# A gated-linear-attention kernel with a SoLU feed-forward: z in natural column order for four chunks, a row-permuted second copy of w_out, two raw weight buffers, and a new written order

## The chip, the cores and the metric

One core of a Trainium2 chip runs the whole kernel. The metric is the time of one execution on the device in microseconds (us), the median of several runs. Lower is better.

## The reference, cut to what matters

Inputs q, k, v, a_re and a_im have the shape (4, 8, 768, 48): 4 sequences (batch), 8 heads, 768 time steps, 48 values per head. The first half is a recurrence with a complex gate whose modulus is cut at 0.999; y of all heads, 384 wide, is the input x of a feed-forward with d_ff = 1024:

```
S_re, S_im = new_re + kv, new_im            # new = a_n * S, kv = outer(k_t, v_t)
y[t] = q_t @ S_re
...
h = x @ w_in                                # (3072, 384) @ (384, 1024)
sm = exp(h - max) / sum(exp(h - max))
solu = h * sm
ln = (solu - mean) / sqrt(var + 1e-06) * g_ln
out = ln @ w_out                            # (3072, 1024) @ (1024, 384)
```

The weights arrive as 64-bit numbers and are turned into fp32 in the kernel.

## The kernel before, in words

**Tiling.** The 3072 rows are 24 chunks of 128 rows: 6 stretches of time by 4 sequences, so chunks 0 to 3 are the first stretch. Two chunks make a group (12 groups). A helper closure exists for each small step of each group or chunk, and the string ORDER (L517) is a list of them, "step:number", written out by hand. The program walks through that list (L1314) and issues each step's instructions. No scheduler moves anything afterwards, so ORDER fixes the sequence of every engine and of the DMA queue of SyncE (SP), which issues nearly all transfers. An instruction waits only for what it reads, and for the buffer that it overwrites to be free.

**Steps of a group** (prep_steps): load_ar and load_ai; inverse, ratio, sure, tangent, square, secant, fourth, size, eps, lnm take the logarithm of the modulus and the tangent of the angle by turns on ScalarE (ACT) and VectorE (DVE); group 0 does each of them in two halves, a and b. total0/1 are products with a triangle of ones (running sums over time, tile f_L); grow and decay are their exponentials; a table load ("trig"), angle, phase0/1 (products again), nearest, part, cos and sin follow, then a table load back ("exp"). From group 3 on the products use a high and a low part in fp32r: lh and ll for total, xh and xl for phase. "on" adds the phase of the stretch before, which "onward" sends over as a transfer, and "last" sends the last row of decay to f_rows.

**Steps of a chunk:** ks and qs scale k and q; k2 and q2 double them with cos and sin; then they are transposed: for chunks 0 and 1 by the tensor engine (kt, qt, copied back by kT, qT), for the rest by DVE in 32x32 blocks (kqb) and four transfers (kqt0). score0/1, mask0 and values give y, carry and add update the state. turned_x copies y; up0/1 are the product with w_in (48 instructions, L1115); exp0 (L1125) writes z = exp(h) from the PSUM tile f_h; solu0 (L1134) multiplies it by h and sums it; centred, spread and norm make mean and variance; z is transposed; down0/1 (L1192) are the product with w_out; scale and store finish.

**The order of z's columns.** For most chunks z is transposed by DVE in 32x32 blocks (blocks, L1152) and by four transfers, one for each block of 32 rows (away, L1157), which spread 32 partitions by 4 column blocks over 128 partitions. So partition p = 4f + s of the result holds column 32s + f of a block of 128. The rows of w_out have to lie the same way: fetch (L742) loads them permuted, and "gain" loads g_ln permuted with four transfers. For the chunks in SHORT (0, 1, 2 and 23) z is transposed whole by the tensor engine (zt, copied by zT), so there exp0 writes z itself in the permuted order: column 32s + f goes to place 4f + s. Then solu0 is four instructions with 256 columns each and centred adds up four sums.

**Weights.** There are 7 pieces: 0 to 2 of w_in (1024 columns each), 3 to 6 of w_out (2 x 384 columns). fetch loads a piece into a buffer of the pool f_raw (3 buffers), raised (ACT, L748) and convert (DVE, three instructions from L754) make fp32 of it, with a tile "bits" between them. mean, meansum and centre fold g_ln and a mean into w_out. "again" loads each piece a second time at the end for inspect (L761), which looks at its smallest size; judge, judgew, judges and count (L1271) make a flag of all checks, and if it isn't zero a general version (function general) runs afterwards. It did not run here. Low parts ll and xl also take buffers of f_raw.

## Time and profile before

| | us |
|---|---|
| median of 3 runs | 418.93 |
| lowest and highest | 418.43 and 420.42 |
| the profiled execution, its own time | 420.45 |
| the profiled execution, first to last instruction (span) | 418.5 |
| tensor engine (PE) busy | 380.5 |
| DVE busy | 341.9 |
| ACT busy | 303.4 |
| GpSimd (POOL) busy | 79.3 |

A row of the profile names the line, the engine, the operation, and the tiles as out<-in; x24 is the number of instructions; then follow the busy time, the mean of one in ns, and the idle time of the engine ahead of it with what ended it. In the timeline the first column is the start, the second the length. PEld is the load of weights into the tensor engine, SPq the issue of a transfer on SP. Matmuls of fp32 count twice, since each is issued as two.

### The profile page before, as it was taken

The numbers are of one execution on the slowest core, as the hardware profiler recorded it, in microseconds if no ns is written. First come the engines' busy times: TensorE is split into PE (matmuls) and PEld (weight loads), VectorE is DVE, ScalarE is ACT, GpSimd is POOL, SyncE is SP. The second block draws the span as 40 slices with busy tenths as digits, with TensorE's granted clock in tenths as the row PEclk, the third lists the DMA queues.
The fourth block names the chain that finished last, engine by engine and source line by source line (L and its number), as shares of the span: only waits on it lengthen the run. The fifth ranks groups of instructions, "written<-read, shape, count | busy, mean of one in ns | idle before, by whom it ended". The sixth has DMA issues, their size and how long they took to land.

```text
span 418.5 us, 15922 instructions
## 1 busy us (share of the span) xinstructions
PE 380.5 (91%) x6968; PEld 206.0 (49%) x6968; DVE 341.9 (82%) x438; ACT 303.4 (73%) x487; POOL 79.3 (19%) x148
## 2 busy tenths in 40 slices
PE   0258769999999999999999999999999999999993
PEld 0026234534655645654654744645645646545552
DVE  4898799888898898898888899989989887963441
ACT  5997887796796887787788778877877967721440
POOL 3000000313222122131122232212304122110110
PEclk9999999999999999999999999999999999999998
DMA  8998338596678667877788858778679669478761
GB/s 228 283 268 227 66 77 172 121 238 125 157 143 185 167 141 144 216 164 146 178 192 186 191 110 198 177 183 207 145 181 211 133 142 217 94 181 258 218 239 30
DMA packets 167406, 72.60 MB, mean 173 GB/s; under 512 B 142496, under 2 KB 155936, under 8 KB 166560
## 3 DMA queue, kind: packets, MB, share of 16 engines
q1 hardware_dynamic: 167040, 71.07, 71.5%
q8 instruction: 57, 0.93, 1.0%
q10 hardware_dynamic: 288, 0.43, 0.3%
q14 instruction: 21, 0.17, 0.1%
HBM read 38.87 MB, written 4.72 MB: 104 GB/s over the span
## 4 chain that ended last, share of the span: by engine, by line
PE 79%; ACT 7%; DVE 5%; DMA 5%; SPq 2%; issue 1%; ACTq 0%; DVEq 0%
PE f_h L1115 27%; PE f_o L1192 25%; PE f_y L1074 9%; PE f_score L1041 6%; PE f_d L1082 3%; DMA out_dram<-f_ot 2%; PE f_L L863 2%; PE f_phase L863 2%; PE f_o L1202 1%; DVE f_kb L996 1%; DVE f_z L1134 1%; PE f_phase L868 1%; DMA f_ar<-in_a_re_dram 1%; PE f_turned L1008 1%; DMA f_k<-in_k_dram 1%
## 5 line engine op out<-in xcount | busy, mean ns | idle before, releaser
L1115 PE MATMUL f_h<-f_w_in,f_xT 128*32 128x512 f32 x1152 | 131.8, 598 | 0.0
L1192 PE MATMUL f_o<-f_w_out,f_zT 128*32 128x384 f32 x1472 | 124.1, 487 | 0.1
L1192 PEld LDWEIGHTS f_o<-f_w_out,f_zT 128*32 128x32 f32 x1472 | 50.8, 110 | 63.1 <-issue 61.8
L1115 PEld LDWEIGHTS f_h<-f_w_in,f_xT 128*32 128x32 f32 x1152 | 40.2, 111 | 66.0 <-issue 65.5
L996 DVE STREAM_TRANSPOSE f_kb<-f_kq 128x1536 f32<-128x1536 f32 x22 | 56.2, 2555 | 0.8 <-DMA f_kqT<-f_kb 0.3
L1125 ACT ACTIVATE f_z<-f_h 128x1024 f32<-128x1024 f32 x24 | 28.8, 1202 | 25.8 <-PE f_h L1115 25.6
L1134 DVE SCALAR_TENSOR_TENSOR f_z<-f_h,f_z 128x1024 f32<-128x1024 f32 (+1 forms) x36 | 33.8, 970 | 11.8 <-ACT f_z L1125 11.6
L1179 POOL TENSOR_SCALAR f_s<-f_s,f_sum 128x1 f32<-128x1 f32 x24 | 12.9, 537 | 149.6 <-ACT f_z L1173 149.5
L1074 PE MATMUL f_y<-f_att,f_v 128*32 128x128 f32 (+1 forms) x384 | 37.0, 278 | 1.1 <-DVE f_att L1046 1.1
L1074 PE MATMUL f_y<-f_att,f_vr 128*32 128x128 f32 x384 | 37.3, 278 | 0.0
L1046 DVE TENSOR_TENSOR f_att<-f_score,f_mats 128x1024 f32<-128x1024 f32 x24 | 29.2, 1215 | 9.7 <-PE f_score L1041 9.7
L1041 PEld LDWEIGHTS f_score<-f_kqT 96*32 96x32 f32 x1536 | 32.2, 112 | 8.2 <-issue 8.1
L1041 PE MATMUL f_score<-f_kqT 96*32 96x32 f32 (+3 forms) x1536 | 33.2, 238 | 0.0
L1074 PE MATMUL f_y<-f_kqT,f_state 96*32 96x128 f32 (+1 forms) x640 | 33.1, 272 | 0.0
L1173 ACT ACTIVATE f_z<-f_z,f_less 128x1024 f32<-128x1024 f32 x24 | 27.3, 1138 | 0.0
L856 POOL TENSOR_TENSOR f_ll<-f_lr,f_lh 128x768 fp32r<-128x768 f32 x9 | 16.6, 1848 | 55.0 <-ACT f_lh L851 48.2
L1074 PEld LDWEIGHTS f_y<-f_att,f_v 128*32 128x32 f32 (+1 forms) x384 | 23.1, 105 | 7.1 <-issue 4.3
L1074 PEld LDWEIGHTS f_y<-f_att,f_vr 128*32 128x32 f32 x384 | 23.2, 112 | 4.8 <-issue 4.8
L1152 DVE STREAM_TRANSPOSE f_zb<-f_z 128x1024 f32<-128x1024 f32 x20 | 24.7, 1237 | 0.1
L1219 ACT ACTIVATE f_ot<-f_o,f_rs 128x384 f32<-128x384 f32 x23 | 13.1, 571 | 14.6 <-PE f_o L1192 6.5
L987 DVE TENSOR_TENSOR f_kq<-f_cs,f_k 128x768 f32<-128x768 f32 x24 | 22.9, 952 | 0.4 <-ACT f_cs L941 0.2
L987 DVE TENSOR_TENSOR f_kq<-f_cs,f_q 128x768 f32<-128x768 f32 x24 | 22.9, 953 | 0.0
(116 smaller groups left out, 628.5 us busy)
## 6 DMA issues: line engine op xcount, KB each, us to landing
f_kqT<-f_kb SPq DMA_DIRECT2D x88, 192.0 KB, 3.3
f_zT<-f_zb SPq DMA_DIRECT2D x80, 128.0 KB, 3.0
f_raw<-in_moe_w_out_dram SPq DMA_DIRECT2D x16, 384.0 KB, 4.6
f_raw<-in_moe_w_in_dram SPq DMA_DIRECT2D x6, 1024.0 KB, 7.9
f_k<-in_k_dram SPq DMA_DIRECT2D x12, 384.0 KB, 5.2
f_q<-in_q_dram SPq DMA_DIRECT2D x12, 384.0 KB, 4.6
f_v<-in_v_dram SPq DMA_DIRECT2D x12, 384.0 KB, 5.4
out_dram<-f_ot SPq DMA_DIRECT2D x23, 192.0 KB, 3.2
```

What stands on the lines that cost most here:

```text
L863: nc.tensor.matmul(out=ps, lhsT=tri.bitcast(FR), rhs=st[nm][:, i * DM:(i + 1) * DM], start=(k == 0), stop=(k == len(parts) - 1))
L987: nc.vector.tensor_tensor(out=t, in0=T["cs", g][:, i * H:(i + 1) * H], in1=heads(T[nm, g][:, i]).unsqueeze(2).to_broadcast([P, H, 2, D]), ...
L996: nc.vector.transpose(out=t, in_=T["kq", c].rearrange("p n h (f j) -> p j (n h) f", j=3))
L1041: nc.tensor.matmul(out=scores[r0:r0 + 32, x, r:], lhsT=QK[:, r // 32, x], rhs=QK[:, r // 32:, H + x], start=True, stop=True)
L1046: nc.vector.tensor_tensor(out=st["att"].rearrange("p (i u) t -> p i u t", u=2), in0=scores.rearrange("p (i u) t -> p i u t", u=2), in1=mat ...
L1074: nc.tensor.matmul(**product)
L1115: nc.tensor.matmul(out=st["h"][r:r + 32, half * 512:(half + 1) * 512], lhsT=st["xT"][:, c * P + r:c * P + r + 32], rhs=w_in[:, c, half * 5 ...
L1125: nc.scalar.activation(out=z, in_=h, func=AF.Exp, accum_out=sums[:, n:n + 1])
L1134: nc.vector.scalar_tensor_tensor(out=z, in0=h, scalar=1.0, in1=z, op0=OP.mult, op1=OP.mult, accum_out=st["sum"][:, 2 + i:3 + i])
L1152: nc.vector.transpose(out=st["zb"], in_=st["z"].rearrange("p (c s f) -> p s c f", s=4, f=32))
L1173: nc.scalar.activation(out=st["z"], in_=st["z"], func=AF.Square, bias=st["less"], accum_out=st["sum"][:, 1:2])
L1192: nc.tensor.matmul(out=st["o"][rows], lhsT=zT, rhs=w_out[:, c], start=(c == 0), stop=(c == KF - 1))
```

## The change

- exp0, solu0 and centred have one form for all chunks: z is in natural order.
- w_out and g_ln are loaded in natural order (g_ln with one transfer). After centring, "mixed" copies w_out in two halves, four transfers each, from SBUF to SBUF into a new tile w_mix with its rows permuted. down uses w_out for the chunks in SHORT, w_mix for the others.
- f_raw has 2 buffers instead of 3. The first loads of pieces 0 and 3 go to the memory of w_mix instead, before it has its own content. The pool "bits" is gone: the bits lie in the tile zb. The low parts ll and xl lie in the tile "f", which the phases of the group also use. judge writes its comparison in place.
- ORDER is another list: the same steps and the two of mixed, in another sequence. Its name init:0 stands for nothing. The tiles of the last down have another name.

The diff; ORDER, which changes as a whole, is cut to its start, a middle piece and its end.

```diff
@@ -514,91 +514,91 @@
 ORDER = """
-load_ara:0 inversea:0 load_aia:0 ratioa:0 surea:0 load_arb:0 tangenta:0 inverseb:0 squarea:0 load_aib:0 secanta:0
-fourtha:0 ratiob:0 sureb:0 sizea:0 fetch:5 epsa:0 tangentb:0 squareb:0 secantb:0 lnma:0 fetch:1 raised:5 load_k:0
-sizeb:0 fetch:0 epsb:0 total0:0 convert:5 load_q:0 fourthb:0 raised:1 grow0:0 decay0:0 lnmb:0 total1:0 grow1:0 fetch:2
-decay1:0 convert:1 trig:0 anglea:0 angleb:0 ks1:0 phase0:0 phase1:0 load_vr:0 raised:0 convert:0 nearest0:0 nearest1:0
-load_ar:1 part0:0 cosa:0 sina:0 qs0:0 qs1:0 load_ai:1 part1:0 ks0:0 sinb:0 fetch:6 cosb:0 q2:0 last:0 exp:0 qt0:0
-qT0:0 raised:2 k2:0 qt1:0 qT1:0 kt0:0 kt1:0 load_v:0 q2:1 convert:2 kT0:0 inverse:1 fetch:3 fetch:4 gain:0 kT1:0 qt1:1
...
-store:20 spread:22 up1:23 inspect:3 norm:22 down0:22 exp0:23 down1:22 again:2 again:1 solu0:23 zt0:23 centred:23
-scale:22 zT0:23 zt1:23 spread:23 down0:23 norm:23 judges:0 zT1:23 inspect:1 store:21 inspect:2 down1:23 scale:23
-store:22 store:23 inspect:4 judgew:0 down2:23 count:0 scale2:23 store2:23 flag:0
+init:0 load_aia:0 load_ara:0 inversea:0 load_arb:0 ratioa:0 load_aib:0 surea:0 load_q:0 tangenta:0 fetch:5 fetch:1
+inverseb:0 squarea:0 ratiob:0 secanta:0 sureb:0 sizea:0 load_v:0 tangentb:0 epsa:0 load_k:0 lnma:0 squareb:0 secantb:0
+fourthb:0 sizeb:0 total0:0 epsb:0 fourtha:0 raised:5 lnmb:0 decay0:0 grow0:0 total1:0 grow1:0 decay1:0 fetch:0 trig:0
+anglea:0 convert:5 phase0:0 last:0 raised:1 qs0:0 angleb:0 convert:1 phase1:0 nearest0:0 part0:0 turn_ends:0
+nearest1:0 ks0:0 ks1:0 sina:0 cosa:0 load_ai:1 qs1:0 part1:0 q2:0 tot:0 sinb:0 k2:0 cosb:0 exp:0 qt1:0 load_ar:1 qT1:0
+raised:0 q2:1 kt1:0 k2:1 convert:0 kT1:0 inverse:1 ratio:1 kt0:0 qt0:0 qT0:0 kT0:0 fetch:2 score1:0 fetch:6 qt0:1
+qT0:1 load_vr:0 score0:0 qt1:1 sure:1 raised:2 load_q:1 mask0:0 values:0 tangent:1 kt1:1 fetch:3 square:1 secant:1
+turned_x:0 convert:2 qT1:1 up0:0 fetch:4 raised:6 size:1 eps:1 convert:6 lnm:1 fourth:1 onward:0 up1:0 gain:0 total1:1
+load_k:1 kT1:1 raised:3 exp0:0 grow1:1 total0:1 decay0:1 grow0:1 carry:1 convert:3 solu0:0 decay1:1 trig:1 angle:1
+kt0:1 phase1:1 ks1:1 qs0:1 kT0:1 add:1 phase0:1 ks0:1 score1:1 raised:4 nearest0:1 score0:1 nearest1:1 convert:4
+part0:1 carry:0 part1:1 mean:0 mean:3 mean:7 add:0 sin:1 cos:1 mask0:1 load_q:2 q2:2 k2:2 mean:1 zt0:0 exp:1 load_ar:2
+mean:4 mean:2 inverse:2 values:1 mean:5 kqb:2 turned_x:1 load_ai:2 ratio:2 mean:6 zT0:0 meansum:0 again:5 last:1
...
+load_ar:3 decay1:2 kqb:3 trig:2 mixed:1 zt0:1 kqt0:3 last:2 values:2 angle:2 spread:0 zT0:1 on:2 phase1:2 ks1:2 norm:0
+qs0:2 turned_x:2 phase0:2 carry:2 load_ai:3 nearest1:2 nearest0:2 up0:2 part1:2 part0:2 sin:2 add:2 cos:2 ks0:2 k2:4
...
+store:18 down0:21 spread:21 solu0:22 again:0 values:23 inspect:4 down1:21 turned_x:23 up0:23 centred:22 up1:23 norm:21
+blocks:22 scale:21 away:22 again:2 down0:22 judge:0 exp0:23 store:21 inspect:0 again:6 spread:22 solu0:23 norm:22
+down1:22 zt0:23 zt1:23 judges:0 inspect:2 inspect:6 scale:22 zT0:23 judgew:0 centred:23 zT1:23 store:20 count:0 flag:0
+spread:23 down0:23 down1:23 norm:23 store:22 scale:23 store:23 down2:23 scale2:23 store2:23
 """
@@ -639,7 +639,7 @@
     const, ld, ldv = pool("f_const", 1), pool("f_ld", 2), pool("f_ldv", 3)
     tmp, one, two = pool("f_tmp", 1), pool("f_one", 1), pool("f_two", 2)
     natk, kbp = pool("f_natk", 2), pool("f_kb", 1)
-    rawp, bits = pool("f_raw", 3), pool("f_bits", 1)
+    rawp = pool("f_raw", 2)
     ffp, zp, sml = pool("f_ff", 2), pool("f_z", 2), pool("f_sml", 4)
     zbp = pool("f_zb", 1)
     ps_t = pool("f_ps_t", 2, space=PSUM)
@@ -654,6 +654,8 @@
     unit, quarter, small, mhalf, magic, mmagic, mone = (bias[:, i:i + 1] for i in range(7))
     w_in = const.tile([P, KD, FF], FP, name="f_w_in")
     w_out = const.tile([P, KF, DM], FP, name="f_w_out")
+
+    w_mix = const.tile([P, KF, DM], FP, name="f_w_mix")
     g_ln = const.tile([P, KF], FP, name="f_g_ln")
 
     state = [const.tile([D2, H // 2, P], FP, name=f"f_state{b}") for b in range(B)]
@@ -672,6 +674,8 @@
     least = const.tile([P, 7], FP, name="f_least")
     T, steps = {}, {}
 
+    EARLY = [0, 3]
+
     SHORT_KQ = [0, 1]
 
     SHORT = [0, 1, 2, 23]
@@ -732,19 +736,19 @@
 
         def fetch(i):
             w, wide, c, per, n = pieces[i % len(pieces)]
-            raw = T["raw", i] = rawp.tile([P, NW, 2], I32, tag="raw", name="f_raw")[:, 0:n]
+            if i in EARLY:
+                raw = w_mix.rearrange("p c x -> p (c x)")[:, 0:2 * NW].bitcast(I32).rearrange("p (n u) -> p n u", u=2)[:, 0:n]
+            else:
+                raw = rawp.tile([P, NW, 2], I32, tag="raw", name="f_raw")[:, 0:n]
+            T["raw", i] = raw
             for k in range(per):
-                rows = wide[:, c + k]
-                if w is w_out:
-
-                    rows = rows.rearrange("(s f) x -> f s x", s=4)
                 m = n // per
-                nc.sync.dma_start(out=raw[:, k * m:(k + 1) * m].rearrange("p n u -> p (n u)"), in_=rows)
+                nc.sync.dma_start(out=raw[:, k * m:(k + 1) * m].rearrange("p n u -> p (n u)"), in_=wide[:, c + k])
 
         def raised(i):
 
             n = pieces[i][4]
-            y = T["bits", i] = bits.tile([P, NW], I32, tag="bits", name="f_bits")[:, 0:n]
+            y = T["bits", i] = zbp.tile([P, NW], FP, tag="zb", name="f_bits")[:, 0:n].bitcast(I32)
             nc.scalar.activation(out=y, in_=T["raw", i][:, :, 0].bitcast(U32), func=AF.Copy, scale=2.0 ** -29)
 
         def convert(i):
@@ -782,7 +786,16 @@
             nc.vector.scalar_tensor_tensor(out=w_out[:, c], in0=w_out[:, c], scalar=g_ln[:, c:c + 1], in1=T["mean"],
                                            op0=OP.mult, op1=OP.subtract)
 
+        def mixed(half):
+
+            cs = slice(half * KF // 2, (half + 1) * KF // 2)
+            for s in range(4):
+                nc.sync.dma_start(out=w_mix[s:P:4, cs].rearrange("p c x -> p (c x)"),
+                                  in_=w_out[s * 32:s * 32 + 32, cs].rearrange("p c x -> p (c x)"))
+
         own = len(pieces)
+        for half in range(2):
+            steps["mixed", half] = partial(mixed, half)
         for i in range(own):
             steps["fetch", i], steps["again", i] = partial(fetch, i), partial(fetch, own + i)
             steps["raised", i], steps["convert", i] = partial(raised, i), partial(convert, i)
@@ -851,11 +864,11 @@
             nc.scalar.activation(out=t, in_=st[src], func=AF.Copy, scale=by)
 
         def low(nm, src, hi, by):
-            t = st[nm] = rawp.tile([P, 1024], FR, tag="raw", name="f_" + nm)
+            t = st[nm] = one.tile([P, GW], FR, tag="f", name="f_" + nm)
             if by == 1.0:
-                nc.gpsimd.tensor_tensor(out=t[:, 0:GW], in0=st[src], in1=st[hi].bitcast(FP), op=OP.subtract)
+                nc.gpsimd.tensor_tensor(out=t, in0=st[src], in1=st[hi].bitcast(FP), op=OP.subtract)
             else:
-                nc.vector.scalar_tensor_tensor(out=t[:, 0:GW], in0=st[src], scalar=by, in1=st[hi].bitcast(FP), op0=OP.mult,
+                nc.vector.scalar_tensor_tensor(out=t, in0=st[src], scalar=by, in1=st[hi].bitcast(FP), op0=OP.mult,
                                                op1=OP.subtract)
 
         def halves(ps, i, *parts):
@@ -1120,19 +1133,12 @@
         def exp():
             z = st["z"] = ffp.tile([P, FF], FP, tag="z", name="f_z")
             h = st["h"]
-            if n in SHORT:
-                z, h = z.rearrange("p (c f s) -> p c s f", s=4, f=32), h.rearrange("p (c s f) -> p c s f", s=4, f=32)
             nc.scalar.activation(out=z, in_=h, func=AF.Exp, accum_out=sums[:, n:n + 1])
 
         def solu():
-            st["sum"] = sml.tile([P, 6], FP, tag="sum", name="f_sum")
-            parts = [(st["h"], st["z"])]
-            if n in SHORT:
-                parts = [(st["h"].rearrange("p (c s f) -> p s c f", s=4, f=32)[:, s],
-                          st["z"].rearrange("p (c f s) -> p s c f", s=4, f=32)[:, s]) for s in range(4)]
-            for i, (h, z) in enumerate(parts):
-                nc.vector.scalar_tensor_tensor(out=z, in0=h, scalar=1.0, in1=z, op0=OP.mult, op1=OP.mult,
-                                               accum_out=st["sum"][:, 2 + i:3 + i])
+            st["sum"] = sml.tile([P, 2], FP, tag="sum", name="f_sum")
+            nc.vector.scalar_tensor_tensor(out=st["z"], in0=st["h"], scalar=1.0, in1=st["z"], op0=OP.mult, op1=OP.mult,
+                                           accum_out=st["sum"][:, 0:1])
 
 
         def turn_z(half):
@@ -1148,7 +1154,7 @@
 
 
         def blocks():
-            st["zb"] = zbp.tile([P, 4, KF, 32], FP, tag="zb", name="f_zb")
+            st["zb"] = zbp.tile([P, FF], FP, tag="zb", name="f_zb").rearrange("p (s c f) -> p s c f", s=4, f=32)
             nc.vector.transpose(out=st["zb"], in_=st["z"].rearrange("p (c s f) -> p s c f", s=4, f=32))
 
         def away():
@@ -1162,12 +1168,7 @@
 
         def centred():
             st["less"] = sml.tile([P, 1], FP, tag="less", name="f_less")
-            total = st["sum"][:, 2:3]
-            if n in SHORT:
-                half, total = st["sum"][:, 2:4], st["sum"][:, 0:1]
-                nc.gpsimd.tensor_tensor(out=half, in0=half, in1=st["sum"][:, 4:6], op=OP.add)
-                nc.gpsimd.tensor_tensor(out=total, in0=st["sum"][:, 2:3], in1=st["sum"][:, 3:4], op=OP.add)
-            nc.gpsimd.tensor_scalar(out=st["less"], in0=total, scalar1=-1.0 / FF, scalar2=None, op0=OP.mult)
+            nc.gpsimd.tensor_scalar(out=st["less"], in0=st["sum"][:, 0:1], scalar1=-1.0 / FF, scalar2=None, op0=OP.mult)
 
         def spread():
             nc.scalar.activation(out=st["z"], in_=st["z"], func=AF.Square, bias=st["less"], accum_out=st["sum"][:, 1:2])
@@ -1185,16 +1186,16 @@
                 st["o"] = ps_o.tile([P, DM], FP, tag="o", padded_shape=[P, 512], name="f_o")
             for c in range(half * KF // 2, (half + 1) * KF // 2):
                 if n in SHORT:
-                    parts = [(slice(r * 32, r * 32 + 32), st["zT"][:, c, r * 32:r * 32 + 32]) for r in range(4)]
+                    parts, w = [(slice(r * 32, r * 32 + 32), st["zT"][:, c, r * 32:r * 32 + 32]) for r in range(4)], w_out
                 else:
-                    parts = [(slice(r * 32, r * 32 + 32), st["zT"][:, r, c]) for r in range(4)]
+                    parts, w = [(slice(r * 32, r * 32 + 32), st["zT"][:, r, c]) for r in range(4)], w_mix
                 for rows, zT in parts:
-                    nc.tensor.matmul(out=st["o"][rows], lhsT=zT, rhs=w_out[:, c], start=(c == 0), stop=(c == KF - 1))
+                    nc.tensor.matmul(out=st["o"][rows], lhsT=zT, rhs=w[:, c], start=(c == 0), stop=(c == KF - 1))
 
         def down_last(part):
 
             if part == 0:
-                st["o"] = [pl.tile([P, DM // 2], FP, tag=tag, padded_shape=[P, 512], name="f_o") for pl, tag in ((ps_o, "o"), (ps_y, "y"))]
+                st["o"] = [pl.tile([P, DM // 2], FP, tag=tag, padded_shape=[P, 512], name="f_" + tag) for pl, tag in ((ps_o, "o"), (ps_y, "y"))]
             for x in ((0, 1), (0,), (1,))[part]:
                 cols = slice(x * DM // 2, (x + 1) * DM // 2)
                 for c in range(KF // 2) if part == 0 else range(KF // 2, KF):
@@ -1245,13 +1246,11 @@
     def judge():
 
         good = sml.tile([P, 2, NG + 1], FP, tag="good", name="f_good")
-        ends = rawp.tile([P, 512, 2], I32, tag="raw", name="f_ends").bitcast(FP).rearrange("p n u -> p (n u)")
-        ends = ends[0:GH, 0:NG * D].rearrange("p (g d) -> p g d", d=D)
         row = one_row()
         nc.vector.tensor_scalar(out=good[:, 0], in0=seen[:, 0], scalar1=MOST, scalar2=None, op0=OP.is_le)
         nc.vector.tensor_scalar(out=good[:, 1], in0=seen[:, 1], scalar1=SURE, scalar2=None, op0=OP.is_le)
         nc.vector.memset(row[:, 3:4], 0.0)
-        nc.vector.tensor_scalar(out=ends, in0=rows[:, :, 0], scalar1=LEAST, scalar2=None, op0=OP.is_ge, op1=OP.add,
+        nc.vector.tensor_scalar(out=rows[:, :, 0], in0=rows[:, :, 0], scalar1=LEAST, scalar2=None, op0=OP.is_ge, op1=OP.add,
                                 accum_out=row[0:GH, 3:4])
         nc.vector.tensor_reduce(out=row[:, 0:1], in_=good.rearrange("p a b -> p (a b)"), op=OP.add, axis=AX.X)
 
@@ -1299,8 +1298,7 @@
         for own in (turn_steps(c), chunk_steps(c), ffn_steps(c)):
             steps.update({(nm, c): f for nm, f in own.items()})
     def gain():
-        for s in range(4):
-            nc.sync.dma_start(out=g_ln[s:P:4], in_=moe_g_ln.rearrange("(c s f) -> f s c", s=4, f=32)[:, s])
+        nc.sync.dma_start(out=g_ln, in_=moe_g_ln.rearrange("(c p) -> p c", p=P))
 
     steps["gain", 0] = gain
     steps["judge", 0], steps["judgew", 0], steps["judges", 0] = judge, judge_weights, judge_sums
```

## The prediction

> **What bounds the kernel now.** I first read the share of each engine in 40 slices, then the busy time in stretches of 10 us, then the waits, and last the timelines of the first 106 us and the last 40. The slices show three parts:
>
> ```profile
> PE   0258769999999999999999999999999999999993
> DVE  4898799888898898898888899989989887963441
> ACT  5997887796796887787788778877877967721440
> ```
>
> TensorE (PE) is filled from the eighth slice to the last but one; before that VectorE (DVE) and ScalarE (ACT) are the full ones. In stretches (columns: length, then busy us of PE, PE loads, DVE, ACT, POOL, clock, DMA share, GB/s):
>
> ```profile
> 0.00:10.00 10.00, 0.00 (x0) 0.00 (x0) 4.10 (x16) 5.17 (x10) 3.48 (x11) 1.00 0.85 221
> 10.00:20.00 10.00, 3.02 (x16) 0.40 (x16) 8.01 (x12) 8.96 (x19) 0.00 (x0) 1.00 0.95 274
> 20.00:30.00 10.00, 5.29 (x27) 2.62 (x28) 9.57 (x14) 9.08 (x15) 0.00 (x0) 1.00 1.12 290
> ...
> 50.00:60.00 10.00, 6.29 (x178) 4.61 (x182) 8.82 (x19) 9.25 (x15) 0.61 (x3) 1.00 0.41 83
> 60.00:70.00 10.00, 8.93 (x131) 3.56 (x127) 9.89 (x12) 7.15 (x14) 0.00 (x0) 1.00 0.49 110
> ...
> 90.00:100.00 10.00, 8.58 (x142) 3.88 (x134) 7.31 (x14) 7.76 (x13) 3.95 (x6) 1.00 0.85 177
> 100.00:150.00 50.00, 50.00 (x980) 27.11 (x974) 44.23 (x53) 40.53 (x65) 11.06 (x18) 1.00 0.67 152
> ```
>
> Adding the ten stretches to 100 us, PE is idle for 31 us; from 100 to 406 it isn't idle at all. The change adds no matmul and takes none away. So it can win only in the start and the tail, and can lose anywhere. What it takes out is in these groups and, in the timeline, in the exp of chunk 1 and of chunk 3:
>
> ```profile
> L1134 DVE SCALAR_TENSOR_TENSOR f_z<-f_h,f_z 128x1024 f32<-128x1024 f32 x20 | 24.4, 1218 | 4.1 <-ACT f_z L1125 3.9
> L1134 DVE SCALAR_TENSOR_TENSOR f_z<-f_h,f_z 128x256 f32<-128x256 f32 x16 | 9.4, 661 | 7.6 <-ACT f_z L1125 7.6
> ...
> 72.23 2.14 ACT L1125 ACTIVATE f_z<-f_h 128x1024 f32<-128x1024 f32 x1
> ...
> 103.94 1.02 ACT L1125 ACTIVATE f_z<-f_h 128x1024 f32<-128x1024 f32 x1 [0.67 <-PE f_h L1115]
> ```
>
> The same exp takes twice as long when z is written four floats apart, and solu is four pieces of 661 ns instead of one of 1218.
>
> **What the Trainium skill says.** "SBUF — State Buffer", section Door 1, has 16-byte lines: an access that crosses to a new line pays, so 4 floats is the limit of a free stride. The trace agrees: 2.14 against 1.02 us. "VectorE: DVE Perf Modes", section The TRN2 errata, gives (N+151)/0.96 ns for fp32 with two tensors: 1224 ns at N=1024, where the trace has 1218; at 256 it gives 424 and the strided pieces take 661. "TensorE: Matmul & The Clock Gate", section What's actually happening, has an idle array run at half rate until some 3.4 us of work. The clock column stays at 1.00, but the durations agree: 8 pieces of f_L take 1.51 us at 12.73, 16 take 1.46 at 47.29.
>
> **The change, part by part.**
>
> Natural order in chunks 0, 1, 2 and 23: exp loses 2.1-1.02 = 1.1 us of ACT each; solu from first start to last accumulator is 2.33 us at 76.64, against 1.23 for one piece at 389.61, so 1.1 us of DVE each; POOL loses two sums of about 0.3 us. Over chunks 0 to 2 that is 3.3 us of ACT and 3.3 of DVE, in a start where both are 70 to 99% busy; part of it is then taken by the next wait.
>
> The row-permuted copy: 8 transfers of 192 KB between SBUF tiles on SP. Nearest row: the kqT transfers, 192 KB in four issues of about 0.63 us (2.56 us at 62.41), landing in 3.3. So some 5 us of SP time and, at 200 GB/s, 8 us of DMA. It first matters for down of chunk 3, after 110 us; half 1 is issued after the last centring (70.1 us now), half 0 behind kqt0 of chunk 4. Cover: SP stands idle from 70.1 to 75.3, and the kqt0 behind it waits for DVE anyway. Bounds: 0, and 2 us if kqT of chunk 3 came late; I take 0.
>
> One tile "f" for low parts and phases: ll now waits for onward of the group before, nearest for both phase products. Now onward of group 3 is issued at 125.27 (2.4 us to land) and ll of group 4 starts at 133.04: 5.4 us in hand. The second phase product comes 0.45 us after the first, and the cos of group 3 ends 16 us ahead of its first scores (117.7 against 134.0). Bounds 0 and 0.45 us for each of 9 groups; I take 0.
>
> bits in the zb tile: already one buffer. Judge in place: 0. Gain in one transfer instead of four: 1024 pieces of 4 bytes both ways; between 0.6 (one issue) and 2.6 us (all four now) of SP.
>
> Raw ring of 2, w_mix as staging for pieces 0 and 3, and the new order: for these I walked the written order of each engine with durations from the timeline, each step starting when its engine is free and its inputs are there. The milestones, with the time now in brackets:
> - a_re is fetched second. Now the first lands at 4.77; 192 KB at 225 GB/s follow in 0.9, so inverse starts at 5.5 (4.80).
> - ACT and DVE then alternate on the two halves. convert:5 (0.55+0.96+0.96 us of DVE) is no longer ahead of lnmb, but fourth, sure and secant are ahead of epsb: second total 16.05 (16.83), trig table done 19.9 (20.63), phase 20.45 (21.23).
> - convert:5 and convert:1 (2.5 and 3.1 us) come ahead of part0, but the latter waits for raised:1 anyway; q2:0 at 25.45 (26.16), table done 28.4 (28.76).
> - Then ACT alternates copies of 0.58, raised:0 (1.15) and inverse:1 (1.7): last kT0 copy 33.5. With PE cold as now (32 score pieces 1.3 us, four turns 0.9) score0 ends at 35.7, mask 36.95, values start 37.0 (37.72); turned_x:0 waits for square and secant, 39.6 (39.80).
> - up:0 40.1 to 46.85, exp:0 contiguous, done 48.05 (49.4). angle:1 at 51.05 (52.38): gain 1.3. raised:4 and convert:4 stand behind it, so the cos ends at 57.6 (58.13), meansum is at 62.05 (62.45).
> - carry:0 and turn_ends:1 no longer stand between meansum and up:1: 62.5 (63.95). Scores of chunk 2 end at 69.7 (71.1).
> - solu0:1 ends at 75.7 (78.97), but kqb:3 now comes behind it; on:2 at 78.0 (79.30), phase:2 at 79.05 (80.33).
> - From its end, 80.5, PE has, without a gap: carry 0.8, up 2.6, zt 0.55, up 2.6, scores 1.15, down 2.6, ends 0.2, values 1.2, down 2.6, carry 0.8, up 5.2, zt 1.1, scores 1.1 = 22.5, so 103.0 plus 0.15 for turned_x:3. Now these scores end at 104.98: 1.8 us gained. Now PE stands twice in this stretch, 0.97 for carry:3 and 0.45 at 97.49, where zt:2 waits for solu0:2; the walk has solu0:2 done at 92.6 (97.4). phase:3, at 111.2 (112.96), keeps the gain.
> If PE is warm from 31 to 46 us, the walk gives 2.8. The new order is about as sparse there, so cold is nearer; I take 2.2 and keep both.
>
> The tail: solu of chunk 23 ends at 402.5 instead of 404.8, but zt comes behind down of chunk 22 (PE free at 405.0), and down:23 behind the copy that follows scale:22: nothing gained. count now stands ahead of down:23 on PE and waits for the last look at the weights; down:23, two scales and two stores wait behind it. Last pieces: again:2 (1 MB) and again:6 (0.8 MB) from about 395.5; now 2 MB issued at 396.2 are in by 405.7. So 404.5, 1.0 for the look, 0.4 for the row: 405.9, ahead of 406.4. Bounds 0 and 2 us; I take 0.
>
> The sum: 2.2 us off the profiled execution's span, 418.5 to 416.3, its time 420.45 to 418.25. That execution is 1.52 us above the median of 418.93; I forecast on the median: 416.7.
>
> **The rivals.** *More is gained* (0.2): the exp and solu saving of chunks 0 to 2 passes through whole, 3.3 us of DVE, and carry out of the way of up:1 adds 1.5: about 5 us, 414. For: DVE at 9.89 of 10 us from 60 to 70. Against: the chain there alternates between ACT, DVE and PE, so each saving meets another wait.
>
> *Given back in the start* (0.12): a_re second costs 0.7, q and v ahead of the weights delay convert, raised:4 late; 419. For: DMA share 0.85 to 1.24 in the first 30 us. Against: the weights still land 3 us ahead of use in the walk.
>
> *Slower* (0.18): SP is held by the ring of 2. fetch:4 must wait for convert:2, which the walk ends at 41.0. Behind it stand onward, gain, load_k:1, load_q:2 and both loads of group 2. Two fetches 1.2, onward 0.6, gain 0.6: load_k:1 at 43.4, where it now goes out at 35.3. Landing takes 5.2 in the median, 8.5 at most, so 48.6 to 51.9, or 54 with a slow gain. ks1:1 wants it at 49.25, and qs, ks, convert:4, part0 stand behind it on DVE, scores of chunk 1 behind those. At 51.4 the gain is gone; at 54 the kernel is 2.5 us slower, 421.4. Against: the DMA share fell to 0.51 by 44 us. That the order does nothing isn't possible: every queue is rearranged.
>
> **How the numbers follow.** A measurement of this kernel tells about 0.5% (2.1 us) from no change. The likeliest case has 0.5, with 414.5 to 418.5 as its own range: 0.29 of it below 416.8, the rest within. Faster by over 0.5% is that 0.29 and the 0.2: 0.49. Slower is the slow rival beyond 421.0 with a small part for stalls of the tile "f": 0.17. Within: 0.34. The range reaches from most of the faster rival into the slow one, whose upper end it leaves out: 412.2 to 421.5.
>
> **What would show it.** Right: exp about 1.03 us and solu 1.22 for all 24 chunks; phase:2 near 79, scores of chunk 4 ending near 103, PE gapless afterwards, the same 5 us of down:23 at the end. Wrong: a wait of ks1:1 for f_k; ll or the products waiting for f_on; a gap of PE at count; any idle PE between 110 and 400, where I have none.

## The result, and the profile after

The kernel after takes 416.15 us in the median of 8 runs (415.10 to 417.58), the kernel before, run beside it, 418.94 (8 runs, 417.62 to 420.42). The ratio is 0.9939, with a 95% interval of 0.9916 to 0.9961: 0.6% faster. The forecast was 416.7. The profiled execution took 415.10 us, with a span of 413.1; that of before had 418.5. These two differ by 5.4 us, almost twice what the medians do, and much of what follows is to find out why.

The slices of the page of after, and its groups of exp and solu:

```profile
PE   0368779999999999999999999999999999999995
DVE  3798999779799899898899889988988988855530
ACT  4997977977887777887877976877976967721332
...
L1140 DVE SCALAR_TENSOR_TENSOR f_z<-f_h,f_z 128x1024 f32<-128x1024 f32 x24 | 29.1, 1213 | 13.5 <-ACT f_z L1136 13.5
...
L1136 ACT ACTIVATE f_z<-f_h 128x1024 f32<-128x1024 f32 x24 | 24.4, 1018 | 21.0 <-PE f_h L1128 21.0
```

PE is full from the seventh slice on, as it was before (the prediction counted that slice as the eighth). All 24 exps now take 1018 ns in the mean, and all 24 solus 1213; the strided forms are gone. The stretches (columns as in the prediction):

```profile
50.00:60.00 10.00, 7.51 (x181) 4.43 (x173) 9.31 (x12) 8.85 (x14) 0.00 (x0) 1.00 0.53 137
60.00:70.00 10.00, 10.00 (x149) 4.11 (x153) 9.92 (x16) 6.13 (x10) 0.00 (x0) 1.00 0.65 141
...
90.00:100.00 10.00, 9.76 (x174) 4.64 (x170) 7.16 (x9) 6.43 (x11) 2.03 (x2) 1.00 0.75 171
100.00:150.00 50.00, 49.84 (x1008) 27.44 (x1000) 44.27 (x53) 41.26 (x67) 8.96 (x20) 1.00 0.78 175
```

From 60 to 70 PE has no idle time (1.07 us before), from 90 to 100 0.24 us (1.42 before). But from 100 to 150 there is a hole of 0.16 us that before did not have. The timeline of PE has the milestones, first before, then after:

```profile
21.23 2.79 PE L868 MATMUL f_phase<-f_x,f_mats 128*32 128x384 f32 x16 [2.89 <-ACT f_x L909]
...
40.70 6.77 PE L1115 MATMUL f_h<-f_w_in,f_xT 128*32 128x512 f32 x48
...
112.89 0.44 PE L863 MATMUL f_phase<-f_xh,f_mats 128*128 128x384 f32 x1
```

```profile
20.55 3.00 PE L881 MATMUL f_phase<-f_x,f_mats 128*32 128x384 f32 x16 [2.83 <-ACT f_x L922]
...
39.13 5.36 PE L1128 MATMUL f_h<-f_w_in,f_xT 128*32 128x512 f32 x48 [1.21 <-ACT f_xT L1121]
...
108.59 0.45 PE L876 MATMUL f_phase<-f_xh,f_mats 128*128 128x384 f32 x1
```

phase:0 is 0.68 us earlier than before, and up:0 starts 1.57 us earlier. It then takes 5.36 us instead of 6.77, so it is 3.0 us ahead at its end. phase:3 is 4.3 us ahead. From there to the start of down:23, 402.50, nothing more is won: 293.91 us against 293.52. From the start of down:23 to the end of the span it is 10.6 us against 12.1. So the profiled pair says 4.3 in the start, 0.4 lost in the middle, and 1.5 won behind the last product. The prediction had 2.2, 0 and 0.

### The profile page after: what moved, and what is told of

Read it like the earlier page. It is cut to its first block, busy times and chain, and to the rows that moved or that the text cites. A ratio compares the mean times of both kernels' runs of the same rounds, so it can differ in the third digit from the quotient of the medians.

```text
span 413.1 us, 15874 instructions
## 1 busy us (share of the span) xinstructions
PE 379.1 (92%) x6968; PEld 202.7 (49%) x6968; DVE 337.0 (82%) x414; ACT 299.0 (72%) x487; POOL 64.5 (16%) x140
## 4 chain that ended last, share of the span: by engine, by line
PE 81%; ACT 8%; DVE 5%; DMA 2%; issue 1%; SPq 1%; DVEq 0%; ACTq 0%
PE f_h L1128 28%; PE f_o L1193 27%; PE f_y L1087 9%; PE f_score L1054 7%; PE f_d L1095 3%; PE f_L L876 2%; PE f_phase L876 2%; DMA f_q<-in_q_dram 1%; DMA f_ar<-in_a_re_dram 1%; ACT f_cs L951 1%; PE f_y L1203 1%; PE f_o L1203 1%; ACT L986 1%; ACT L989 1%; DVE f_kb L1009 1%
## 5 line engine op out<-in xcount | busy, mean ns | idle before, releaser
L1193 PE MATMUL f_o<-f_w_mix,f_zT 128*32 128x384 f32 x1280 | 108.6, 487 | 0.0
L1193 PEld LDWEIGHTS f_o<-f_w_mix,f_zT 128*32 128x32 f32 x1280 | 42.8, 110 | 54.1 <-issue 51.5
L1140 DVE SCALAR_TENSOR_TENSOR f_z<-f_h,f_z 128x1024 f32<-128x1024 f32 x24 | 29.1, 1213 | 13.5 <-ACT f_z L1136 13.5
L1180 POOL TENSOR_SCALAR f_s<-f_s,f_sum 128x1 f32<-128x1 f32 x24 | 11.7, 485 | 182.1 <-ACT f_z L1174 181.9
L1136 ACT ACTIVATE f_z<-f_h 128x1024 f32<-128x1024 f32 x24 | 24.4, 1018 | 21.0 <-PE f_h L1128 21.0
L1087 PE MATMUL f_y<-f_att,f_v 128*16 128x128 f32 (+1 forms) x384 | 36.7, 273 | 0.8 <-DVE f_att L1059 0.8
L1054 PE MATMUL f_score<-f_kqT 96*32 96x64 f32 (+3 forms) x1536 | 34.0, 238 | 0.0
L1087 PEld LDWEIGHTS f_y<-f_att,f_v 128*32 128x32 f32 (+1 forms) x384 | 22.0, 103 | 7.5 <-issue 6.4
L1087 PEld LDWEIGHTS f_y<-f_att,f_vr 128*32 128x32 f32 x384 | 22.3, 109 | 1.7 <-issue 1.7
L1171 POOL TENSOR_SCALAR f_less<-f_sum 128x1 f32<-128x1 f32 x24 | 6.3, 266 | 88.7 <-DVE f_z L1140 88.7
```

What stands on the lines that cost most here:

```text
L1054: nc.tensor.matmul(out=scores[r0:r0 + 32, x, r:], lhsT=QK[:, r // 32, x], rhs=QK[:, r // 32:, H + x], start=True, stop=True)
L1087: nc.tensor.matmul(**product)
L1136: nc.scalar.activation(out=z, in_=h, func=AF.Exp, accum_out=sums[:, n:n + 1])
L1140: nc.vector.scalar_tensor_tensor(out=st["z"], in0=st["h"], scalar=1.0, in1=st["z"], op0=OP.mult, op1=OP.mult, accum_out=st["sum"][:, 0:1])
L1193: nc.tensor.matmul(out=st["o"][rows], lhsT=zT, rhs=w[:, c], start=(c == 0), stop=(c == KF - 1))
```

## The experiments

All traces are read by the same four numbers: the start and length of up:0, then the starts of phase:3 (the end of the start) and of down:23, then the span. All kernels, in us; the last two columns are what was timed, the median of several runs and its ratio to the kernel before, timed beside it. The kernel before had 417.68 to 418.94 in the four series, so ratios are compared rather than medians of different series. The traces show one execution each:

| kernel | up:0 | phase:3 | down:23 | span | median | ratio |
|---|---|---|---|---|---|---|
| before | 40.70, 6.77 | 112.89 | 406.41 | 418.5 | 418.94 | 1 |
| e11_before_again | 39.40, 5.36 | 110.96 | 404.76 | 416.7 | 418.45 | 0.9996 |
| e5_before_warm | 38.31, 5.36 | 111.21 | 405.65 | 417.6 | 418.39 | 1.0020 |
| after | 39.13, 5.36 | 108.59 | 402.50 | 413.1 | 416.15 | 0.9939 |
| e7_after_again | 39.17, 5.47 | 109.44 | 404.31 | 414.7 | 415.99 | 0.9937 |
| e1_old_order | 38.37, 5.36 | 107.87 | 406.46 | 418.4 | 421.90 | 1.0116 |
| e8_old_order_own_low | 40.56, 6.91 | 111.15 | 404.49 | 416.5 | 416.88 | 0.9960 |
| e10_old_order_own_low_tail | 39.60, 5.36 | 109.11 | 402.50 | 412.8 | 414.89 | 0.9900 |
| e9_new_order_own_low | 39.16, 5.36 | 109.43 | 403.90 | 414.4 | 415.95 | 0.9930 |
| e2_strided_z | 39.20, 5.36 | 112.34 | 408.88 | 419.3 | 421.36 | 1.0096 |
| e3_count_last | 38.92, 5.36 | 108.38 | 403.14 | 415.3 | 417.21 | 0.9954 |
| e12_strided_last | 38.67, 5.36 | 109.86 | 404.64 | 415.1 | 416.90 | 0.9950 |
| e4_are_first | 38.03, 5.36 | 107.50 | 402.03 | 412.5 | 415.07 | 0.9901 |
| e6_after_warm | 40.39, 5.33 | 109.95 | 404.00 | 414.6 | 416.69 | 0.9973 |

The theory at the outset: the shorter exp and solu and the new order share the gain, in the start, and it came out larger than predicted as PE ran at full rate from 34 us on. The rivals: the columns alone, the order alone, or the end of the program.

**1. The code without the order (e1_old_order).** The kernel after, with ORDER from before, apart from the two steps of mixed and the second reading of the weights, which the changed code needs elsewhere:

```
-ORDER: init:0 load_aia:0 load_ara:0 inversea:0 ... zT1:23 store:20 count:0 flag:0 spread:23 ...
+ORDER: load_ara:0 inversea:0 load_aia:0 ratioa:0 ... kqb:3 mixed:1 ... lh:3 mixed:0 ... down2:23 count:0 ...
```

> The changed code in the old written order (the row copy of the weights put behind kqb of chunk 3 and lh of group 3, the second looks at the weights as in the new order, since the ring of 2 needs them there). The kernel before takes 418.9, the kernel after 416.15. My theory (code and order share the gain, the order has the larger part, through the start): 417.5 to 418.3, phase:2 about 79.5 to 80. Rival A, the natural column order is the whole gain: 416.2, phase:2 near 76.5. Rival B, the order is the whole gain: 418.9, or more if the ring of 2 makes the loads wait in the old order.

Measured: 421.90 us (6 runs), ratio 1.0116 (1.0077 to 1.0155), slower than before. My theory and rival A missed in time; rival B's "or more" came true, but through the tile f, not through the ring of 2. Rival A's other sign did come: phase:2 is at 76.75, where the kernel after has 76.53. In the start the old order with the changed code is as quick as the new one; its phase:3, 107.87, is the earliest but one of all. It loses 4.8 us between there and 354 us. The waits of this kernel, then PE and POOL at the sums of group 8, where the high part's product is done and the low part's isn't there:

```profile
POOL f_ll L870 <- DMA f_on<-f_f: 47.3, 6, 8.4
```

```profile
252.64 0.44 PE L877 MATMUL f_L<-f_lh,f_mats 128*128 128x384 f32 x1
253.98 0.45 PE L877 MATMUL f_L<-f_ll,f_mats 128*128 128x384 f32 x1 [0.90 <-POOL f_ll L870]
```

```profile
252.11 1.81 POOL L870 TENSOR_TENSOR f_ll<-f_lr,f_lh 128x768 fp32r<-128x768 f32 x1 [8.26 <-DMA f_on<-f_f]
```

POOL had stood for 8.26 us, until the transfer "onward" of the group before had read the tile f, which is now also the tile of ll. SP had issued it only at 248.56. In the kernel after it is issued at 241.17, and ll follows lh instead:

```profile
248.56 0.60 SPq L959 DMA_DIRECT2D f_on<-f_f  x1
```

```profile
241.17 0.69 SPq L958 DMA_DIRECT2D f_on<-f_f  x1
...
249.14 1.86 POOL L869 TENSOR_TENSOR f_ll<-f_lr,f_lh 128x768 fp32r<-128x768 f32 x1 [5.17 <-ACT f_lh L864]
```

The distance of the two lh products is 0.46 us where nothing waits. In the old order it is 1.47, 0.59, 1.36, 1.62, 0.64, 1.64 and 0.68 in groups 5 to 11: 4.8 us too much.

**2. The same with the low parts in their old tile (e8_old_order_own_low), and the new order with it (e9_new_order_own_low).**

```
-            t = st[nm] = one.tile([P, GW], FR, tag="f", name="f_" + nm)
+            t = st[nm] = rawp.tile([P, 1024], FR, tag="raw", name="f_" + nm)[:, 0:GW]
```

> The changed code in the old written order as in the run of the old order, but the low parts in the raw ring again instead of the tile of the phases. There the wait of the low parts for the transfer of the phases kept the two halves of the sums apart by 1.47, 0.59, 1.36, 1.62, 0.64, 1.64 and 0.68 us where 0.46 is the rule, 4.8 us in all. My theory (this wait is what the new order avoids, and the natural columns are the gain): 4.8 us less than the old order had, 1.0116 to 1.000, and the span of the profiled run 413.5 to 414.5. Rival A (the wait moves on to the next wait): 1.006 to 1.012. Rival B (the old order without the wait is as good as the new): 0.993 to 0.996.

> The kernel after with the low parts in the raw ring again. The trace of the kernel after has 0.46 us between the halves in every group, so nothing is there to be won: the same as after, within 0.2%. Rival (the shared tile holds up something in the new order, too): 0.5 to 1 us faster than after.

Measured: the old order goes from 421.90 to 416.88 us (22 runs), ratio 0.9960 (0.9941 to 0.9978): 5.0 us by the medians, 6.5 by the ratios. In the traces the stretch from phase:3 to down:23 goes from 298.59 to 293.34 us, so the 4.8 us come back. The ratio lies between the theory and rival B. The span of 416.5 missed the 413.5 to 414.5, since up:0 ran half cold in this execution (experiment 4). Its waits:

```profile
POOL f_ll L870 <- ACT f_lh L865: 44.2, 7, 7.1
```

In the new order the edit does nothing, as expected: 415.95 (8 runs) against 415.99. So the shared tile is free in the new order and costs some 5 us in the old one. That is the main thing the new order does for this change.

**3. Strided z in the new order (e2_strided_z), and in the last chunk alone (e12_strided_last).** exp, solu and centred as before, for the chunks in SHORT, or for chunk 23:

```
+            if n in SHORT:        # e12: if n == 23
+                z, h = z.rearrange("p (c f s) -> p c s f", s=4, f=32), h.rearrange("p (c s f) -> p c s f", s=4, f=32)
             nc.scalar.activation(out=z, in_=h, func=AF.Exp, accum_out=sums[:, n:n + 1])
```

> The new order with the old strided z in the four chunks (exp writes four floats apart, solu in four pieces, two more sums on GpSimd). w_out stays in natural order, so the columns of z of these four chunks meet the wrong rows of w_out. My theory: the strided forms cost 1.1 us of ScalarE and 1.1 us of VectorE per chunk in a start where about half passes through: 417.3 to 418.3, solu of chunk 1 ends at 75 to 76 instead of 73.0. Rival A (natural order is the whole gain): 418.9 or more. Rival B (the order is the whole gain): 416.2.

> The kernel after with strided z in chunk 23 alone, so that the columns of z of this chunk meet the wrong rows of w_out. In the kernel after the row for count is there at 401.4, 1.1 us ahead of count on TensorE (402.5). The strided exp is 1.1 us longer and solu 1.4, and the last look at the weights stands behind them: the row comes 1.4 us too late, and the turned z waits too: 1.4 to 2.4 us slower than after, 0.997 to 0.9995 of before. Rival (the prediction's: the last chunk's columns gain nothing, as zt comes behind down of chunk 22 anyway): the same as after, 0.9935.

Measured: 421.36 us (6 runs), ratio 1.0096 (1.0065 to 1.0127), more than my theory had; solu of chunk 1 ended at 75.89, as expected. Against e7_after_again, phase:3 is 2.9 us later, and down:23 another 1.7, as PE waits 1.72 us at count. In the last chunk the row of the checks now comes too late. In e12_strided_last, DVE and then PE:

```profile
404.33 0.16 DVE L1272 TENSOR_REDUCE f_row<-f_fine 128x1 f32<-128x7 f32 x1
...
404.64 0.17 PE L1282 MATMUL f_count<-f_row,f_mats 128*1 128x4 f32 x1 [1.51 <-DVE f_row L1272]
```

and in the kernel after:

```profile
401.24 0.16 DVE L1260 TENSOR_REDUCE f_row<-f_fine 128x1 f32<-128x7 f32 x1
```

```profile
402.50 0.17 PE L1270 MATMUL f_count<-f_row,f_mats 128*1 128x4 f32 x1 [0.26 <-ACT f_zT L1153]
```

There the row is ready at 401.40, 1.1 us ahead; with strided z PE stands for 1.51 us, down:23 behind it. The trace shows the expected wait; the time does not settle it: 0.9950 (0.9930 to 0.9971) is below the expected 0.997, and its interval holds the rival's 0.9935.

**4. The rate of PE in the start (e5_before_warm, e6_after_warm, e11_before_again).** The first two add products that nobody reads where PE is idle:

```
+    def warm():
+        ps = ps_o.tile([P, DM], FP, tag="o", padded_shape=[P, 512], name="f_warm")
+        for r in range(0, P, 32):
+            nc.tensor.matmul(out=ps[r:r + 32], lhsT=ident[:, r:r + 32], rhs=mats[:, 1:4].rearrange("p n t -> p (n t)"),
+                             start=True, stop=True)
```

> The kernel before with eight idle-time products on TensorE whose result nobody reads (three behind the second total of group 0, four behind its phase, one behind tot), each of four matmuls 32x384, about 0.75 us in all when cold. If the gain came largely because TensorE runs at full rate from 34 us instead of from about 43 us, this alone takes values of chunk 0 from 2.0 to 1.3 us and up:0 from 6.77 to about 5.4: 1.5 to 2 us off, 417.0 to 417.4. Rival (the start is bound by ScalarE and VectorE, and a faster TensorE only waits): 418.5 to 419. Rival (the products get in the way): above 419.5.

> The kernel after with nine such products (three behind the second total of group 0, three behind tot, one behind mask of chunk 0, two behind turned_x of chunk 0). If the rate of TensorE sets the stretch from 26 to 36 us, the turns go from 1.09 to 0.64 us and the scores from 1.3 to 0.75: 0.5 to 1 us off, 415.2 to 415.7. Rival (ScalarE's copies of the turned parts set this stretch): 416.15, the same as after.

> The kernel before, unchanged, for a second profile. If its slow up:0 (6.77 us, the first part of it at half rate) belongs to the kernel, it is there again: up:0 from 40.7 in 6.8 us, phase:3 at 112.9. If it comes and goes from run to run in this order, as it did between two kernels with the same start (5.36 us at 38.37 in the old order, 6.91 us at 40.56 in the old order with its own low parts), it may be 5.36 us at 38.4 here and phase:3 near 111.

Measured: e5 418.39 us (14 runs), ratio 1.0020 (1.0006 to 1.0035); e6 416.69 (22 runs), 0.9973 (0.9952 to 0.9993), which is not better than the kernel after (0.9937). Both theories of the gain missed. In e5 up:0 did run at full rate from 38.31, but phase:3 is at 111.21, no better than in the kernel before without the products (110.96). e6 delays phase:0 from 20.5 to 21.34: the products stand in its way. In the trace of e5 PE falls back to half rate twice later on, as shown below. The plain kernel before, traced again, has a quick up:0, and e8 with the old order has a slow one:

```profile
39.40 5.36 PE L1115 MATMUL f_h<-f_w_in,f_xT 128*32 128x512 f32 x48 [0.36 <-ACT f_xT L1108]
```

```profile
40.56 6.91 PE L1129 MATMUL f_h<-f_w_in,f_xT 128*32 128x512 f32 x48
```

So in the old order it comes and goes: slow in before and e8, quick in e1, e10 and e11. In the eight traces of the new order up:0 took 5.33 to 5.47 us. e1 and e8 have the same start in code, and phase:3 is 3.3 us apart in them. That is part of why the profiled pair shows 4.3 us in the start: before was traced with a cold up:0, after was not.

The traces hold records of the granted clock, from which the clock column is made, and these say when PE came to full rate. They begin there, and for the time ahead of the first record the column shows 1.00 whatever the rate was. The first record starts at 43.59 us in before and at 43.74 in e8, inside up:0; at 35.47 in e11, 30.39 in e1, 35.77 in e10 and 34.49 in after, ahead of up:0; at 39.45 in e7, 0.28 us into it. If up:0 takes 5.36 us at full rate and half rate costs half of the time from its start to that moment, before, e8 and e7 should have 6.81, 6.95 and 5.50 us; they have 6.77, 6.91 and 5.47. In the eight traces of the new order PE was at full rate from 39.45 us at the latest; that the order makes it so isn't shown by eight.

The other half of it is a second patch of half rate later on. The stretches of e7_after_again and of after, in the same 5 us:

```profile
50.00:55.00 5.00, 5.00 (x134) 3.02 (x127) 3.74 (x8) 3.25 (x7) 0.00 (x0) 0.69 1.09 280
```

```profile
50.00:55.00 5.00, 4.36 (x136) 2.63 (x128) 4.83 (x8) 4.07 (x8) 0.00 (x0) 1.00 1.05 270
```

The clock of e7 is 0.50 from 50 to 53, and its phase:1 takes longer than that of after, from nearly the same start; phase:2 is then at 77.36 instead of 76.53:

```profile
49.80 2.79 PE L881 MATMUL f_phase<-f_x,f_mats 128*32 128x384 f32 x16 [1.89 <-ACT f_x L922]
```

```profile
49.76 1.50 PE L881 MATMUL f_phase<-f_x,f_mats 128*32 128x384 f32 x16 [1.89 <-ACT f_x L922]
```

e11 has such a patch at 55 to 60 (0.66), e5 two between 49 and 60. Of the fourteen traces only those of before and after, the profiled pair, have none ahead of their end.

The timed runs fit this. In the three later series, 36 executions of the kernel before had a mean granted clock of 0.996 or 0.997: 12 took 415.9 to 417.6 us and 24 took 419.4 to 421.3, with none between. The profiled before (420.45 us, 0.997) lies in the upper group. Where PE came to full rate in the others isn't on record, so that their up:0 was cold is not shown.

**5. The unchanged kernel after once more (e7_after_again).**

> The kernel after, unchanged, as the measure for the others of this call. Against the kernel before in its own comparison: 0.9939. The same is expected, 0.992 to 0.996; if the earlier difference came from one chip only, nearer to 1.

Measured: 415.99 us (15 runs), ratio 0.9937 (0.9917 to 0.9956), as expected. With e11 it makes a second pair of traces, both with a quick up:0 and one patch of half rate: 1.5 us won in the start, 1.1 lost in the middle, 1.6 won at the end, 2.0 in all.

**6. The place of count (e3_count_last), and the new end on the old order (e10_old_order_own_low_tail).**

```
-... zT1:23 store:20 count:0 flag:0 spread:23 ... down2:23 scale2:23 store2:23
+... zT1:23 store:20 spread:23 ... down2:23 count:0 scale2:23 store2:23 flag:0
```

> The kernel after with count and flag behind the last down again. From the start of down:23 to the end of the span the traces show 12.1, 11.9 and 11.9 us where count comes last (the kernel before, the old order, the kernel before with the extra products) and 10.6, 10.6 and 10.4 where it comes ahead. If the place of count does it: 1.3 to 1.5 us slower than after, span 414.5 where after has 413.1. Rival (the end is that of the stores, count doesn't matter): the same as after.

> The old order with the changed code and the low parts in the raw ring (416.88, 0.996 of before), and on top of it the end of the new order: the looks at the last weights, count and flag ahead of the last down. If the place of count is worth the 1.2 us that putting it back cost in the new order: 0.993 to 0.994, the same as after. Rival (the last look at the weights isn't done in time, and TensorE waits at count): 0.996 or more, with a gap at count.

Measured: e3 417.21 us (22 runs), 1.2 more than e7 beside it; it has 12.2 us from the start of down:23 to the end of the span. The end of its timeline, and that of after:

```profile
408.84 0.14 DVE L1275 TENSOR_SCALAR flag<-f_total 1x1 int32<-1x1 f32 x1
409.07 0.38 ACTq L1216 DMA_DIRECT2D out_dram<-f_ot  x1
```

```profile
402.91 0.14 DVE L1275 TENSOR_SCALAR flag<-f_total 1x1 int32<-1x1 f32 x1
...
408.45 0.38 ACTq L1216 DMA_DIRECT2D out_dram<-f_ot  x1
```

From the issue of the last store to the end of the span: 6.2 us with the flag at 408.98, 4.65 with the flag at 403.05. The products and stores of down:23 are equally quick in both, so the difference lies behind the last store: the program's end loads the flag to decide on the general version. Which instruction there takes the time, this profile doesn't list. e10 has 414.89 us (6 runs), 0.9900 (0.9857 to 0.9943), at least as good as expected: the end works on the old order, too, and PE waits there for 0.29 us. With the low parts in their old tile and this end, the old order is as quick as the new one; apart from the tile f and the place of count, no run shows a gain of the new order.

**7. a_re first (e4_are_first).**

```
-init:0 load_aia:0 load_ara:0 inversea:0
+init:0 load_ara:0 load_aia:0 inversea:0
```

> The kernel after with a_re of group 0 fetched ahead of a_im. The prediction priced the swap at 0.7 us of the start (inverse at 4.80 instead of 5.58). If the first chain of group 0 sets the start: phase:0 at about 19.9 instead of 20.55, and 0.3 to 0.7 us faster than after, 0.992. Rival (the weights and q and k behind it set the start from 26 us on): the same as after, 0.9935, with values:0 at 36.1 as now.

Measured: 415.07 us (6 runs), ratio 0.9901 (0.9864 to 0.9938). phase:0 is at 19.53, 1.0 us earlier, up:0 at 38.03, phase:3 at 107.50; nearly all of the 1.0 is kept. The median of e7, from another series, is 0.9 higher. The two best medians, e4 and e10, are below that of after; the intervals of the ratios touch that of after, so the order of the three isn't settled by time alone.

## Why the prediction was right, and where it was wrong

**Natural columns** (1.1 us of ACT and of DVE per chunk, part of it taken by the next wait): right in kind. With nearly equal starts of up:0, from e11 to e10, phase:3 gains 1.85 us; with cold ones, from before to e8, 1.74. That is the whole changed code in the old order, not z alone; from e11 to e1, which has the same start in code as e10, it is 3.1, of which 1.0 lies ahead of up:0. Only e2 changes the form of z alone: against e7, 2.9 us in the new order, from one pair of traces, each with one patch of half rate; the rival *more is gained* had 3.3. One reading of the prediction doesn't hold as it stands: it has a stride of 4 floats as the limit of a free one and says that the trace agrees, but the stride here is just these 4 floats, and exp takes 2.14 us with it and 1.02 without.

**The walk of the start** was good to 0.2 us as far as PE's cold part goes: inverse 5.58 (predicted 5.5), second total 16.22 (16.05), phase:0 20.55 (20.45), q2:0 25.27 (25.45). Further on PE was ahead of the walk: phase:2 76.53 (79.05), scores of chunk 4 done at 100.6 (103.0). "a_re second costs 0.7" was in it; undone, it gave 1.0. The step that failed is "The new order is about as sparse there, so cold is nearer; I take 2.2": PE was at full rate for up:0 in every trace of the new order. For the pair of profiled executions the start gave 4.3, above even the 2.8 for a warm PE. But the kernel before isn't always cold: in the second pair it gave 1.5. The forecast was hung on a single trace, one in which a cold patch had fallen on up:0, and I took the 1.52 us of that execution above the median off the forecast as if both kernels had them. "Measured from the medians" and "measured from one trace" are different gains.

**One tile "f"** (bounds 0 and 0.45 for each of 9 groups; I take 0): right for this kernel, and wrong as an argument. I looked at group 4 of the old order, with 5.4 us in hand, and spoke for all. Groups 5 to 11 of that order lose 4.8 us in all, up to 1.2 in one, beyond my upper bound for a group. The zero holds because the new order issues onward earlier, which I had not worked out.

**The tail** ("nothing gained"): the mis-sized term. The row was predicted 0.5 us ahead of PE, and was 1.1 ahead, so count costs nothing. That it fits is luck: the 406.4 of the sum is down:23 in the kernel before, 404.2 with the forecast 2.2 taken off, which the row of 405.9 would have missed. It came in time because the last two pieces were issued at 390.88 and 392.07, not from 395.5, and had landed by 398.93, not 404.5. And I priced only what the move of count costs. What it gives is 1.2 us in time (e3) and 1.5 in the traces, behind the last store.

**Idle PE between 110 and 400** would show me wrong, I had written. There is some, 0.16 us in after and 0.90 in e7:

```profile
144.18 1.92 PE L1128 MATMUL f_h<-f_w_in,f_xT 128*32 128x512 f32 x16 [0.90 <-issue]
```

Six of the eight traces of the new order have this hole inside up:6, of 0.16, 0.38, 0.44, 0.44, 0.61 and 0.90 us; e6 has one of 0.40 at 264.20 instead; those of the old order have none. "issue" means that nothing in the profile shows what PE waited for. In all seven a 16 KB transfer of the queue listed as "instruction" had begun 2.3 to 2.8 us before PE went on, but each trace has 57 of these, nearly all without a hole behind. The cause is open, and no run was made on it.

**The slow rival** did not come: load_k:1 was issued at 40.83, not 43.4. fetch:4 needs its buffer free when the second instruction of convert:2 has read it (38.72; SP issued at 38.79), and I had counted the third, too, from a later start. ks1:1 ran at 48.02 with no wait. **mixed** took 3.58 and 3.13 us of SP, more than the 5 I had for both, all of it hidden.

The sum: 2.2 + 0 + 0 was forecast, and the medians give 2.8 and 2.4 in two series. In the two pairs of traces it stands as 1.5 to 4.3 in the start, 0.4 to 1.1 lost in the middle, 1.2 to 1.6 won at the end. So the forecast was close in part because a left-out gain and a left-out loss nearly cancel.

## What to carry to other kernels

A change that shares a buffer and reorders the work has to be priced as a pair: run the code in the old order and every group's wait shows, where one group checked by hand does not. A check whose result decides how a program ends can cost time behind the last store; compute it ahead of the last product, if its inputs leave a margin. And before a gain is read off two traces, trace each kernel twice: here one kernel's own start moved by 1.9 us at phase:3 between two executions.

## What was not expected of the hardware

The clock column shows 1.00 in the first 50 us of the kernel before although its first products run at half rate, but 0.50 from 50 to 53 us in e7, where the same products slow down by the same factor. The second is the first kind coming back; the column shows it only once the records of the clock have begun (experiment 4).

The Trainium skill, "TensorE: Matmul & The Clock Gate", section What's actually happening, has a free-running window of 3.4 us that must be busy for the gate to open. The records agree, and with the length: the records are 58 stretches of full or half rate in the fourteen traces, and all of them but the last of each trace, 44, last a whole multiple of 3.413 us. The one of e11, as the column has it (behind the stretch stand its length and PE's busy time; the clock is the third figure from the end):

```profile
52.50:55.90 3.40, 1.52 (x56) 1.25 (x48) 3.31 (x7) 3.26 (x6) 0.00 (x0) 1.00 0.74 138
55.96:59.35 3.39, 3.39 (x46) 2.39 (x39) 3.35 (x3) 3.35 (x5) 0.00 (x0) 0.50 0.00 0
59.40:62.00 2.60, 2.21 (x38) 0.88 (x33) 2.43 (x4) 0.89 (x4) 0.00 (x0) 1.00 0.30 65
```

PE was busy for less than half of the window ahead of the patch, and for all of the patch. Much the same holds throughout, counted to 110 us in all traces: each of the 15 falls to half rate stands behind a window in which PE was busy for 0.76 to 1.73 us, and PE kept its full rate behind no window of less than 1.52. It came to full rate behind windows of 2.86 us at least, and behind all 16 that had no idle time; but it also stayed at half rate behind one of 3.30, so busy time is not all that counts.

This explains the cold up:0. In the kernel before PE was busy from 30.93 to 36.58 us, 5.65 us, and values still ran slowly at 37.72: counted back from 43.59, the windows ended at 33.35, 36.76 and 40.18, and each held a gap (0.44, 0.19 and 0.95 us). The first without one ended at 43.59. In the kernel after the window from 31.08 to 34.49 had none, and the turns were quick at 34.61. Where these edges lie changes from one execution to the next, and with it the start of one and the same program. It also says where the extra products of e5 fell short: they stand ahead of 37 us, and its two falls, at 49.08 and 55.91, come behind windows with 1.45 and 1.73 us of work. This is read from the traces; no run moves the edges on purpose.
